# A conversion moves to the second products, and the last expert's splits, transposes and a table load change places, in an attention, MoE and MLP kernel on one core

## The chip, the cores and the metric

The kernel runs on one core of a Trainium2 chip. The metric is the device time of one execution in microseconds. It is taken from runs without a profile; one further execution is profiled, and all rows come from that one.

## What is computed

```python
kv = np.einsum('bhsd,bhse->bhde', k, v); out = np.einsum('bhsd,bhde->bhse', q, kv)
x = out / sqrt(mean(out * out) + 1e-6) * g_norm          # 2304 tokens x 512
noisy = x @ w_gate + log1p(exp(x @ w_noise)) * noise     # 8 experts
top2 = the two largest of each token; weights by softmax over the two
for e in range(8):
    h = np.maximum(x[mask] @ w1[e], 0)                   # 512 -> 1024
    out[mask] += weight * (h @ w2[e])                    # 1024 -> 512
h = out @ w_in; g = h * sigmoid(h); y = g @ w_out        # 512 -> 2048 -> 512
```

q, k, v and the experts' weights are float32. w_in and w_out are float64.

## The kernel before

There are three phases. The attention and the routing end at some 119 us. The experts run from there to 576.6 us, and the MLP from there to the end.

Each product of the experts and of the MLP is made of three passes over split operands. A split takes a float32 tile, rounds it on ScalarE to a high part (h..., such as hw) and subtracts this on VectorE or GpSimd to get the low part (l..., such as lw). Instructions of TensorE, ScalarE and VectorE go through the helper `InOrder` (line 44 of the listing, hence L44 in nearly all rows), which keeps each of the three engines in the order in which the program is written. SyncE (the queue for loads and most stores) and GpSimd are ordered by the compiler's scheduler.

An expert e has 640 places, in five tiles a = 0 to 4 of 128. Its work has two halves.

- First products, `mm1`, for f = 0 to 7: x times a column block of w1, first for places 0 to 255 (part 0, matrices of 256 columns) and then for places 256 to 639 (part 1, 384 columns), 12 matmuls each. ScalarE then writes the high part of h, VectorE the low part (h<-ph in the rows). Beside it, at odd f, w1 of the next expert is split with the subtraction on GpSimd; at even f a conversion runs.
- Second products, `mm2`, for a = 0 to 4: 24 matmuls py, going over f = 0 to 7 with three passes each; the last of the 24 is the one that reads the low part of h of f = 7. After a tile, ScalarE copies py to y and stores it (`store_y`; tiles 0 and 1 go to y_first too). Then follow, by the tables TURN and SPLIT: transposes of gathered rows for the next expert (`Places.turn`: TensorE, then ScalarE for the high part, VectorE for the low part, xT<-xt in the rows), a split of w2 of the next expert (here on VectorE, lw<-rw), and one conversion. Row tile 4 of the next expert is turned inside tile a = 4, before f = 4.

A conversion (`convert`) turns a 128 x 256 block of float64 of w_in or w_out into float32. It has six VectorE instructions in the order bits, bits, unit, w, f, keep, and two on GpSimd: w<-w,bits (L1097), then w<-w,keep (L1098). A store to win_dram or wout_dram and the load of the next float64 block follow on SyncE. There are 64 conversions. Experts 1 to 6 hold five in the first products (f = 0, 2, 4, and two at f = 6) and five in the second, one behind each tile.

The last expert, 7, has no next expert. It splits the first half of w_in (win, four loads of 512 KB from win_dram) in its first products. Then comes `overflow`, a loop with a run-time count for tokens over an expert's room; here the engines go past it. Then the second half of w_in is fetched through the two raw buffers, and split behind tiles 0 (two), 1 and 2. `Block(0)` is the MLP's first block of 256 rows. Its `fetch` gathers two rows per token from y_first into the same raw buffers; `add` weights and adds them on VectorE, `turn` transposes them on TensorE (x2ps) and `split` makes the two parts (x2T). In expert 7, `add(0)`, `turn(0)`, `split(0)` and `add(1)` are written behind tile 3, and row tile 1 is turned inside tile 4 before f = 6. `load_rt(i)` loads the table of places and weights of block i: 16 bytes for each token.

Of the kernel before, what the change touches and what calls it, by code (L numbers as in the profile page):

```python
# [24 lines left out]


TURN = (((), (), (0, 1), (2, 3), ()), ((0, 1), (2,), (3,), (), ()))
SPLIT = ((0, 0, 2, 1, 1), (1, 1, 1, 1, 0), (2, 1, 1, 0, 0))

LOG = (  # L30
    1.7336119413375854, -2.4589619636535645, 1.9598705768585205, -0.5900887250900269, 0.3407464623451233,
# [16 lines left out]
def attention_moe_mlp(  # L48
# [15 lines left out]
    nc = tc.nc  # L64
    pe, act, dve = (InOrder(tc, engine) for engine in (nc.tensor, nc.scalar, nc.vector))
# [13 lines left out]
    NS = CAP // P  # L79
# [112 lines left out]
    def fetch(src, name, shape, raw=None):  # L192
        if raw is None:
            raw = raw_pool[0].tile([P, 1024], F32, tag="raw", name="r" + name, bufs=2)
        nc.sync.dma_start(raw if shape is None else raw.rearrange("p (a b) -> p a b", a=shape), src)
        return raw

    def split(raw, name, high, low):

        hi = wslot("h" + name)  # L200
        lo = wslot("l" + name)
        high.activation(hi, raw, AF.Copy)
        low.tensor_sub(lo, raw, hi.bitcast(F32))  # L203
        return hi, lo
# [13 lines left out]
    def behind(ins):  # L218
        return tc.issue_after(ins.ins) if ins else ExitStack()
# [91 lines left out]

    raw1, raw2, h0 = [], [], []
    listed, marked, stored = {}, {}, []

    def early_y(a, between):

# [10 lines left out]
    with ExitStack() as ph1:  # L327
# [13 lines left out]
        kv, kvT, qT, raw, ss, rinv, logits = {}, {}, {}, {}, {}, {}, {}  # L341
# [632 lines left out]
    def fetch_win(fh):  # L974
        return [
            (fetch(win_dram[c][:, fh * 1024 : (fh + 1) * 1024], f"win{fh}_{c}", None), f"win{fh}_{c}")
            for c in range(KD)
        ]
# [4 lines left out]
    def load_rt(i):  # L983
        s0, s1 = BLOCKS[i]
        rt = mp.tile([P, 4, 4], F32, tag="rt", name=f"rt{i}", bufs=2)[:, : (s1 - s0) // P, :]
        whole = rt_dram[s0:s1, :].rearrange("(t p) c -> p t c", p=P)
        if i:
            nc.sync.dma_start(rt, whole)
        else:
            first = first_dram[s0:s1, :].rearrange("(t p) c -> p t c", p=P)  # L990
            with behind(stored[-1]):
                nc.sync.dma_start(rt[:, :, :TOP], first.bitcast(F32))
                nc.sync.dma_start(rt[:, :, TOP:], whole[:, :, TOP:])
        return rt
# [51 lines left out]
    with ExitStack() as ph2:  # L1046
        tp = ph2.enter_context(tc.tile_pool(name="tp", bufs=2, reuse_waits="tile"))
        tails[0] = tp

        CW = 256  # L1050
        todo = []
        for s0 in range(0, DFF, CW):
            cols = slice(s0, s0 + CW)
            for c in range(KD):
                todo.append((w_in[c * P : (c + 1) * P, cols], win_dram[c][:, cols]))
        for c in range(KFF):
            for s0 in range(0, DM, CW):
                cols = slice(s0, s0 + CW)
                todo.append((
                    w_out[c * P : (c + 1) * P, cols],  # L1060
                    wout_dram[c // 2][(c % 2) * P : (c % 2 + 1) * P, cols],
                ))
        loaded = []

        def load_next():
            if todo:
                src, dst = todo.pop(0)
                raw = tp.tile([P, CW, 2], I32, name="f64", bufs=3)
                nc.sync.dma_start(raw.rearrange("p a b -> p (a b)"), src.bitcast(I32))
                loaded.append((raw, dst))  # L1070


        def convert():
            if not loaded:
                return
            raw, dst = loaded.pop(0)
            top, low = raw[:, :, 1], raw[:, :, 0]
            bits = tp.tile([P, CW], I32, name="bits", bufs=2)
            dve.tensor_scalar(
                bits, top, 3, 0x3FFFFFFF, op0=ALU.logical_shift_left, op1=ALU.bitwise_and  # L1080
            )
            dve.scalar_tensor_tensor(
                bits, top, -0x40000000, bits, op0=ALU.bitwise_and, op1=ALU.bitwise_or
            )
            unit = tp.tile([P, CW], I32, name="unit", bufs=1)
            dve.tensor_scalar(unit, bits, -0x800000, None, op0=ALU.bitwise_and)
            w = tp.tile([P, CW], F32, name="w32", bufs=4)
            dve.scalar_tensor_tensor(
                w, low.bitcast(U32), 2.0**-52, unit.bitcast(F32), op0=ALU.mult, op1=ALU.mult
            )  # L1090
            dve.tensor_scalar(
                top, top, 20, 0x7FF, op0=ALU.logical_shift_right, op1=ALU.bitwise_and
            )

            keep = tp.tile([P, CW], F32, name="keep", bufs=2)
            dve.tensor_scalar(keep, top, 897.0, None, op0=ALU.is_ge)
            nc.gpsimd.tensor_add(w, w, bits.bitcast(F32))  # L1097
            nc.gpsimd.tensor_mul(w, w, keep)  # L1098
            nc.sync.dma_start(dst, w)
            load_next()  # L1100

        def h_tiles(e, f, n):
            return tuple(
                tp.tile([P, CAP], F32R, tag="h", name=f"h{e}_{f}_{l}", bufs=2 * KF)[:, :n] for l in range(2)
            )

        def places(t, s0):
            return lambda a: tuple(x[:, a * P - s0 : (a + 1) * P - s0] for x in t)

        x = Places(0, range(HA // P, NS))  # L1110
        for a in x.tiles:
            x.fetch(a)
        early_y(1, {a + 2: (lambda a=a: x.turn(a)) for a in x.tiles})
        for e in range(E):
            more = e + 1 < E
            now, x = x, Places(e + 1, range(NS))
            if e == 2:
                n_iter = nc.values_load(ntot[0:1, 0:1], min_val=0, max_val=28)
            raw = fetch_w1(e + 1) if more else fetch_win(0)
            got = []  # L1120
            if e == 0:
                w2_sb[0] = []
            parts = (0, 1) if e else (1,)
            s0 = PARTS[parts[0]][0]
            h = []
            for f in range(KF):
                t = h_tiles(e, f, CAP - s0)
                mm1(e, w1_sb[e], now.parts, f, parts, t)
                h.append(places(t, s0))
                if e == 0 and f == 1:  # L1130
                    tiles()
                if f % 2 == more:
                    got.append(split(*raw.pop(0), act, nc.gpsimd if more else dve))
                elif e == 0:
                    w2_sb[0].append(split(raw2[f // 2], f"w2_0_{f // 2}", act, dve))
                elif more:
                    convert()
                    if f == 6:
                        convert()
                if more and f in (2, 4, 6):  # L1140
                    x.fetch(f // 2 - 1)
            if more:
                w1_sb[e + 1] = got
                raw = fetch_w2(e + 1)
                got = w2_sb[e + 1] = []
            else:
                win.update({(0, c): t for c, t in enumerate(got)})
                overflow(n_iter)
                raw = fetch_win(1)
                got = []  # L1150
            if e == 0:
                for _ in range(3):
                    load_next()
            for a in range(s0 // P, NS):
                between = {}
                if a == NS - 1:
                    between = {4: lambda: x.turn(NS - 1)} if more else {6: lambda: (x.turn(1), x.split(1))}
                mm2(e, w2_sb[e], h, a, between)
                if more:
                    for n in TURN[e > 0][a]:  # L1160
                        x.turn(n)
                        if n < 2:
                            x.fetch(n + 3)
                for _ in range(SPLIT[(e > 0) + (not more)][a]):
                    got.append(split(*raw.pop(0), act, dve))
                convert()
                if not more and a == 1:
                    x = Block(0)
                    x.fetch(0)
                    x.fetch(1)  # L1170
                if not more and a == 3:
                    x.add(0)
                    x.turn(0)
                    x.split(0)
                    x.add(1)
            if not more:
                win.update({(1, c): t for c, t in enumerate(got)})
# [5 lines left out]
    with ExitStack() as ph3:  # L1183
# [70 lines left out]
        for i in range(len(BLOCKS)):  # L1254
# [4 lines left out]
            x = Block(i + 1) if i + 1 < len(BLOCKS) else None  # L1259
# [45 lines left out]
```

## Time and profile before

| | |
|---|---|
| median of three runs | 989.76 us (989.26 to 991.65) |
| the profiled execution, its own time | 992.24 us |
| its span, first to last instruction | 990.4 us |
| mean granted clock of TensorE | 0.99 |

In timelines a row has the start from the beginning of the span, the length, the engine, the line and the operation, what it writes and reads with the buffer numbers left out, how many instructions were merged, and in brackets the idle time of the engine before it with what ended it. An engine name with q is its queue: an issue or a wait, no work. PE is TensorE, DVE VectorE, ACT ScalarE, POOL GpSimd, SP SyncE. The name behind an idle time is inferred from semaphores.

### The profile page before, as it was taken

To read this page: it belongs to the slowest core of one execution; us is meant where nothing else is said; L and a number is where in the kernel's file an instruction comes from. 1 tells how busy PE (TensorE), PEld (TensorE's weight loads), DVE (VectorE), ACT (ScalarE), POOL (GpSimd) and SP (SyncE) were. 2 spreads that over 40 slices of the span, in tenths; PEclk is the share of its full clock that TensorE was granted. 3 is DMA by queue.
4 is the path that set the end of the run, shared out by engine and by line. 5 is a ranking of instruction groups with operands and counts; after the bars stand their busy time and mean duration, and the time that the engine had idled before them with its cause. 6 is when DMAs were issued, how large, how long until landed. Compare 5 with 4: busy or idle time off the path is not lost. (4 is left out here: it accounts for less than half of the span.)

```text
span 990.4 us, 14460 instructions
## 1 busy us (share of the span) xinstructions
PE 958.6 (97%) x5586; PEld 819.8 (83%) x5586; DVE 499.0 (50%) x941; ACT 327.5 (33%) x499; POOL 253.1 (26%) x271
## 2 busy tenths in 40 slices
PE   6989999999999999999999999999999999999998
PEld 5877589889798998979888789888888888888886
DVE  2578657676666667576673355232333332232221
ACT  2765254333323323333333243221321231223212
POOL 3000266445455454544520221001100010100000
PEclk9999999999999999999999999999999999999999
DMA  9861737474755638375561472101110020101001
GB/s 325 302 240 45 256 119 237 156 249 128 240 164 187 212 124 282 127 224 186 159 202 51 162 231 86 43 1 43 49 37 21 23 85 1 43 1 43 0 1 44
DMA packets 65096, 127.01 MB, mean 128 GB/s; under 512 B 11264, under 2 KB 19456, under 8 KB 65024
## 3 DMA queue, kind: packets, MB, share of 16 engines
q1 hardware_dynamic: 49392, 91.33, 28.6%
q0 software_dynamic: 6080, 19.93, 6.5%
q10 hardware_dynamic: 9552, 14.79, 4.1%
q8 instruction: 45, 0.74, 0.3%
q14 instruction: 27, 0.22, 0.1%
HBM read 92.94 MB, written 33.08 MB: 127 GB/s over the span
## 5 line engine op out<-in xcount | busy, mean ns | idle before, releaser
L44 PE MATMUL ph<-xT,hw 128*128 128x256 f32 (+1 forms) x960 | 212.5, 312 | 0.1
L44 PE MATMUL py<-hw,h 128*128 128x512 f32 x608 | 200.9, 402 | 7.6 <-DVE h L44 5.5
L44 PE MATMUL pout<-hwout,g 128*128 128x512 f32 x576 | 191.8, 395 | 0.0
L44 PE MATMUL pg<-x2T,hwin 128*128 128x512 f32 (+1 forms) x640 | 184.2, 373 | 0.0
L44 PEld LDWEIGHTS ph<-xT,hw 128*128 128x128 f32 x960 | 162.6, 189 | 1.8 <-DVE xT L44 0.6
L44 DVE TENSOR_TENSOR sg<-pg,sg 128x512 f32<-128x512 f32 x72 | 49.8, 692 | 211.2 <-ACT sg L44 211.2
L44 PE MATMUL ph<-xT,lw 128*128 128x256 f32 (+1 forms) x480 | 149.8, 312 | 0.0
L44 PEld LDWEIGHTS py<-hw,h 128*128 128x128 f32 x608 | 115.2, 189 | 35.8 <-DVE h L44 8.1
L44 PEld LDWEIGHTS pg<-x2T,hwin 128*128 128x128 f32 x640 | 116.6, 189 | 23.4 <-DVE x2T L44 0.2
L44 PEld LDWEIGHTS pout<-hwout,g 128*128 128x128 f32 x576 | 108.2, 188 | 24.3
L44 PE MATMUL py<-lw,h 128*128 128x512 f32 x304 | 120.5, 396 | 0.0
L44 PE MATMUL pg<-x2T,lwin 128*128 128x512 f32 (+1 forms) x320 | 119.0, 372 | 0.0
L44 ACT ACTIVATE sg<-pg 128x512 f32<-128x512 f32 x72 | 43.0, 597 | 217.6 <-PE pg L44 217.6
L44 PE MATMUL pout<-lwout,g 128*128 128x512 f32 x288 | 112.9, 392 | 0.0
L1014 POOL DMA_INDIRECT yg<-y_dram,rt x32 | 31.9, 996 | 260.8 <-PE x2ps L44 219.8
L44 DVE SCALAR_TENSOR_TENSOR h<-ph,h 128x640 fp32r<-128x640 f32 (+1 forms) x64 | 50.5, 789 | 82.6 <-ACT h L44 78.2
L44 ACT ACTIVATE h<-ph 128x640 fp32r<-128x640 f32 (+1 forms) x64 | 43.5, 680 | 144.3 <-PE ph L44 141.4
L44 PEld LDWEIGHTS ph<-xT,lw 128*128 128x128 f32 x480 | 90.6, 189 | 0.0
L1097 POOL TENSOR_TENSOR w<-w,bits 128x256 f32<-128x256 f32 x64 | 47.3, 740 | 145.0 <-DVE w L44 144.7
L44 DVE TENSOR_TENSOR g<-sg,g 128x512 fp32r<-128x512 f32 x72 | 49.8, 692 | 44.7 <-ACT g L44 44.7
L203 POOL TENSOR_TENSOR lw<-rw,hw 128x1024 fp32r<-128x1024 f32 x28 | 67.5, 2410 | 17.0 <-ACT hw L44 17.0
L44 PEld LDWEIGHTS pg<-x2T,lwin 128*128 128x128 f32 x320 | 60.4, 189 | 11.5
(177 smaller groups left out, 1083.6 us busy)
## 6 DMA issues: line engine op xcount, KB each, us to landing
rw<-in_moe_w_dram SPq DMA_DIRECT2D x56, 512.0 KB, 4.1
y_dram<-y ACTq DMA_DIRECT2D x40, 256.0 KB, 4.4
f<-in_moe_w_in_dram SPq DMA_DIRECT2D x32, 256.0 KB, 3.7
f<-in_moe_w_out_dram SPq DMA_DIRECT2D x32, 256.0 KB, 3.3
k<-in_k_dram SPq DMA_DIRECT2D x16, 288.0 KB, 5.9
v<-in_v_dram SPq DMA_DIRECT2D x16, 288.0 KB, 6.0
q<-in_q_dram SPq DMA_DIRECT2D x16, 288.0 KB, 6.3
out_dram<-ob SPq DMA_DIRECT2D x18, 256.0 KB, 3.3
```

Source lines behind the costliest of these rows:

```text
L44: return lambda *args, **kwargs: self.tc.keep_in_program_order(op(*args, **kwargs))
L203: low.tensor_sub(lo, raw, hi.bitcast(F32))
L1014: nc.gpsimd.indirect_dma_start(out=y, out_offset=None, in_=src, in_offset=bass.IndirectOffsetOnAxis(ap=self.rt[:, t, kk : kk + 1].bitcast( ...
L1097: nc.gpsimd.tensor_add(w, w, bits.bitcast(F32))
```

## The change

In experts 1 to 6 the second conversion at f = 6 of the first products goes. In its place there are two conversions behind tile 3 of the second products. Expert 7's two splits behind tile 0 move into tile 0, before f = 3 and before f = 6. Row tile 0 of the MLP is turned and split inside tile 4 before f = 1, no longer behind tile 3, and row tile 1 before f = 5, no longer f = 6. The loads of rt for blocks 1 and up are ordered on SyncE behind the last fetch of w_in.

```diff
-SPLIT = ((0, 0, 2, 1, 1), (1, 1, 1, 1, 0), (2, 1, 1, 0, 0))
+SPLIT = ((0, 0, 2, 1, 1), (1, 1, 1, 1, 0), (0, 1, 1, 0, 0))
@@ fetch
-        nc.sync.dma_start(raw if shape is None else raw.rearrange("p (a b) -> p a b", a=shape), src)
+        fetched.append(
+            nc.sync.dma_start(raw if shape is None else raw.rearrange("p (a b) -> p a b", a=shape), src)
+        )
@@ load_rt
         if i:
-            nc.sync.dma_start(rt, whole)
+            with behind(last_win[0]):
+                nc.sync.dma_start(rt, whole)
@@ first products
                 elif more:
                     convert()
-                    if f == 6:
-                        convert()
@@ expert 7, behind its first products
                 raw = fetch_win(1)
+                last_win.append(fetched[-1])
@@ second products
                 if a == NS - 1:
-                    between = {4: lambda: x.turn(NS - 1)} if more else {6: lambda: (x.turn(1), x.split(1))}
+                    between = {4: lambda: x.turn(NS - 1)} if more else {
+                        1: lambda: (x.turn(0), x.split(0)), 5: lambda: (x.turn(1), x.split(1))
+                    }
+                elif a == 0 and not more:
+                    between = dict.fromkeys((3, 6), lambda: got.append(split(*raw.pop(0), act, dve)))
                 mm2(e, w2_sb[e], h, a, between)
...
                 convert()
+                if e and more and a == 3:
+                    convert()
...
                 if not more and a == 3:
                     x.add(0)
-                    x.turn(0)
-                    x.split(0)
                     x.add(1)
```

## Rows read from the trace of the kernel before

**Rows 1.** The page's busy times: engine, us, share of span, instructions.
```profile
PE 958.6 (97%) x5586; PEld 819.8 (83%) x5586; DVE 499.0 (50%) x941; ACT 327.5 (33%) x499; POOL 253.1 (26%) x271
```
**Rows 2.** TensorE's waits, 130 to 580 us: total us, times, longest us.
```profile
PE py L44 <- DVE h L44: 5.5, 6, 0.9
PE py L44 <- DMA rt<-rt_dram: 2.1, 1, 2.1
```
**Rows 3.** VectorE's timeline, expert 1, end of its first products.
```profile
182.38 0.28 DVE L44 TENSOR_SCALAR bits<-f 128x256 int32<-128x256 int32 x1
182.70 0.43 DVE L44 SCALAR_TENSOR_TENSOR bits<-f,bits 128x256 int32<-128x256 int32 x1
...
184.79 0.28 DVE L44 TENSOR_SCALAR bits<-f 128x256 int32<-128x256 int32 x1
185.11 0.93 DVE L44 SCALAR_TENSOR_TENSOR bits<-f,bits 128x256 int32<-128x256 int32 x1
...
189.79 0.81 DVE L44 SCALAR_TENSOR_TENSOR h<-ph,h 128x640 fp32r<-128x640 f32 x1
```
**Rows 4.** TensorE's timeline, end of expert 1's first tile of second products.
```profile
189.12 0.40 PE L44 MATMUL py<-hw,h 128*128 128x512 f32 x1
189.36 0.39 PE L44 MATMUL py<-lw,h 128*128 128x512 f32 x1
190.66 0.50 PE L44 MATMUL py<-hw,h 128*128 128x512 f32 x1 [0.91 <-DVE h L44]
```
**Rows 5.** VectorE's timeline, from expert 2's last tile into expert 3.
```profile
272.57 0.28 DVE L44 TENSOR_SCALAR bits<-f 128x256 int32<-128x256 int32 x1
...
275.19 0.74 DVE L44 SCALAR_TENSOR_TENSOR xT<-xt,gcol,xT 128x512 fp32r<-128x512 f32 x1
...
277.86 0.66 DVE L44 TENSOR_SCALAR keep<-f 128x256 f32<-128x256 int32 x1
279.59 0.82 DVE L44 SCALAR_TENSOR_TENSOR h<-ph,h 128x640 fp32r<-128x640 f32 x1 [1.07 <-ACT h L44]
```
**Rows 6.** TensorE's timeline there: the first products that read columns 256 to 639.
```profile
276.54 0.51 PE L44 MATMUL ph<-xT,hw 128*128 128x384 f32 x2
```
**Rows 7.** The same place between experts 0 and 1.
```profile
157.03 0.83 PE L44 MATMUL ph<-xT,hw 128*128 128x384 f32 x2
```
**Rows 8.** GpSimd's timeline beside rows 5.
```profile
275.42 0.74 POOL L1098 TENSOR_TENSOR w<-w,keep 128x256 f32<-128x256 f32 x1 [0.29 <-DVE keep L44]
```
**Rows 9.** Stretches: busy us of PE, PEld, DVE, ACT, POOL; granted clock; DMA share; GB/s.
```profile
544.20:547.60 3.40, 3.40 (x8) 2.66 (x9) 0.82 (x1) 0.00 (x0) 0.00 (x0) 0.50 0.88 269
570.00:573.40 3.40, 3.34 (x17) 2.82 (x18) 1.73 (x4) 0.60 (x1) 0.00 (x0) 1.00 0.81 205
```
**Rows 10.** Timelines behind the spare loop: SyncE's first issue, TensorE's first matmul.
```profile
542.29 0.37 SPq L988 DMA_DIRECT2D rt<-rt_dram  x1
...
544.10 0.75 PE L44 MATMUL py<-hw,h 128*128 128x512 f32 x1 [2.14 <-DMA rt<-rt_dram]
```
**Rows 11.** The table rt from 542 to 620 us: issue to landing of its three loads.
```profile
DMA to landing us min/median/max: 3.3/3.7/6.6
```
**Rows 12.** Expert 7's last tiles: timelines of SyncE, GpSimd, VectorE and TensorE.
```profile
555.37 1.46 SPq L195 DMA_DIRECT2D rwin<-win_dram  x2
...
564.15 0.99 POOL L1014 DMA_INDIRECT yg<-y_first,rt  x1 [4.37 <-issue]
...
564.78 1.23 DVE L44 TENSOR_TENSOR lwin<-rwin,hwin 128x1024 fp32r<-128x1024 f32 x1 [3.22 <-ACT hwin L44]
...
569.25 0.75 DVE L44 SCALAR_TENSOR_TENSOR yg<-yg,rt 128x512 f32<-128x512 f32 x1 [0.93 <-DMA yg<-y_first,rt]
...
572.76 0.75 DVE L44 SCALAR_TENSOR_TENSOR yg<-yg,rt 128x512 f32<-128x512 f32 x1 [0.29 <-DMA yg<-y_first,rt]
...
570.06 0.66 PE L44 MATMUL x2ps<-ident,yg 128*128 128x128 f32 x4 [1.83 <-DVE yg L44]
```
**Rows 13.** The two stores to y_first issued at 552.2 and 557.7: issue to landing.
```profile
DMA to landing us min/median/max: 2.1/3.9/5.6
```

More of the change, by code (lines that the diff above doesn't have):

```diff
@@ L313, in attention_moe_mlp @@
     listed, marked, stored = {}, {}, []
+    fetched, last_win = [], []
     def early_y(a, between):
```

## The prediction

> **What bounds the kernel.** I read the busy times first. TensorE is busy for 958.6 us, 97% of the span; VectorE for half of it [rows 1]. So a change counts only where it takes away or makes an idle stretch of TensorE, and the next view is TensorE's waits. In the experts' phase there are eight: six of 0.9 us on the low part of h, which VectorE writes, one of 2.1 put down to the table rt [rows 2], and one of 1.8 on a sum yg of VectorE [rows 12]. The change touches the places of all eight. The third view is VectorE's timeline around them, because VectorE runs in program order: what is written ahead of the awaited instruction delays it.
>
> **The six waits that the change removes.** In expert 1 the first conversion at f = 6 starts at 182.38, the second at 184.79, and the low part of h of f = 7 at 189.79 [rows 3]. The second conversion thus takes 5.00 us against 2.41 for the first. TensorE goes through tile 0 meanwhile. Its last matmul should start 0.23 behind the one at 189.36, the pace of its neighbours, so at 189.59; it starts at 190.66 [rows 4]. The loss is 1.07 us. Without the second conversion the low part could start some 5 us earlier, ahead of its use by far, so the whole loss goes: 6 x 1.07 = 6.4 us.
>
> **What the moved conversion costs where it lands.** It is written behind tile 3, so it stands in VectorE's queue ahead of the low part of row tile 4 of the next expert, which is turned inside tile 4. That is xT, and TensorE waits for it: the second matmul of part 1 in the next expert's first product reads it. How much room is there? From expert 2 into 3, the conversion behind tile 3 starts at 272.57 and xT at 275.19; xT ends at 275.93 [rows 5]. The first two matmuls of part 1 start at 276.54 and 0.18 later [rows 6], so xT is needed at 276.72. The room is 0.79 us. From expert 0 into 1 there is none left already: the same pair spans 0.83 in place of 0.51 us [rows 6, 7].
>
> A conversion is longer than that room. The one alone takes 2.41 us to the start of the next [rows 3]. One right behind another also meets the GpSimd multiplication of that other one. This ran at 275.42 for 0.74 us [rows 8], and the second instruction of the moved conversion would start at about 275.5, inside it. At f = 6 the same meeting made 0.93 us out of 0.43 [rows 3]. So I take 2.41 + 0.50 = 2.91 us. The trace of before shows no second conversion at this very place, so the bounds are: below, 2.41, no meeting; between, 2.59, what the conversion behind xT takes there, from 275.93 to 278.52 [rows 5]; above, the 5.00 of f = 6. The last is far off, since at f = 6 GpSimd also splits w1, and behind tile 3 the split is VectorE's own. 2.91 stands nearest to what I can see of the place.
>
> With 2.91, xT ends at 278.84. TensorE restarts 0.06 later, as it does at 570.06 behind the sum that ends at 570.00 [rows 12], so at 278.90 and not 276.72: 2.18 us at each of six transitions, 13.1 us. With 2.59 it is 11.2, with 2.41 it is 10.1. Nothing is added behind it: VectorE idles 1.07 us ahead of the next low part of h [rows 5], and that one moves back with TensorE.
>
> The Trainium skill (SBUF — State Buffer, section "Who interferes with whom") says that a VectorE instruction with two SBUF inputs contends with a GpSimd one that reads SBUF, and that the second to issue is blocked until the first ends; one with a single input outside the faster modes is not. Of the first two instructions at f = 6 the one with two inputs was stretched, so the trace agrees. By that rule the sum is the one with 2.91; by the undisturbed row it is that with 2.41.
>
> Net of the two parts: 13.1 - 6.4 = +6.7 us. The float64 load and the store that a conversion issues on SyncE move with it. Three blocks are in flight, so the next conversion's block was asked for two conversions earlier, and I cost them at nothing; that distance hides them, and without it each could cost up to a load's few us. On GpSimd the two instructions of the moved conversion pass no gather that TensorE waits for within 2 us.
>
> **Expert 7.** TensorE starts the transposes of row tile 0 at 570.06, after 1.83 us of idle, because the sum of that tile ends at 570.00 [rows 12]. The sum waits for a gather, and the gather for the store of tile 1 to y_first and for a raw buffer. The two stores to y_first landed after 2.1 and 5.6 us [rows 13]. The second, issued at 557.7, runs beside two fetches of w_in issued from 555.37 [rows 12]; it lands at 563.3, and the first gather starts at 564.15 [rows 12]. With the splits inside tile 0, these fetches go out as soon as the earlier halves have landed and are split, some 4 us sooner, and the second store is alone: it lands near 560, and gathers start from 561. The sum then waits on VectorE for the split that ends at 566.01 [rows 12] and is done by 567.5, before the transposes are reached at 568.8. That takes away the wait of some 2.0 us. The sum of row tile 1 now ends at 573.51 [rows 12] and needs a gather that still starts behind 566.01, so I move it up by under a microsecond, to 572.6. TensorE gets there at 571.9, earlier than now, and waits 0.7. Gain 2.0 - 0.7 = 1.3 us. If the store lands no sooner, only the moved places count, 0.6; at most it is 2.0. The two splits now sit ahead of ScalarE's copy of tile 0, some 7 us behind the restart at 544.10 [rows 10]; their loads are issued at once behind the loop, so they should be done by then. If not, the copy and its store are late, which costs at most what is gained here.
>
> **The table load.** The wait of 2.1 us is put down to rt [rows 2], and the stretch behind it runs at a granted clock of 0.50 for 3.40 us [rows 9], which costs 1.7 more. But rt is issued at 542.29 [rows 10] and the quickest of these loads lands after 3.3 us [rows 11], so at 545.6 or later, and TensorE is back at 544.10 [rows 10]. The label is a coincidence; what ends there is the way past the loop. I cost the move of rt at nothing: it is now queued on SyncE behind w_in's fetches, and its first user, block 1, is more than 20 us away.
>
> The Trainium skill (Runtime: NRT & Kernel Launch, section "Instruction fetch mechanics") says that a taken branch to code outside the fetched pages waits for a load of that code. By that rule too the move gains nothing; were the label right, it would gain 3.8.
>
> **The clock.** The idle stretch of 2.14 us was followed by half clock [rows 9, 10], the lower of the two levels, 1.2 in place of 2.4 GHz; that of 1.83 us was not [rows 9, 12]. My new waits would show as about 2.0 us (278.90 less the end of the matmul before, 276.88), between the two. Each that falls on the wrong side costs 3.40 x 0.5 = 1.7 us. The rows don't say where the limit lies, so I count none or one of six in the forecast and leave more to a rival.
>
> **The sum.** +6.7 - 1.3 = +5.4 us, with one stretch at half clock +7.1. The profiled execution has its own time of 992.24, 2.5 above the median of 989.76; the difference goes on the median: 995.2 to 996.9. I predict 996.0 us. Alone, this case reaches from 993 to 999.
>
> **Rivals.** The wait is hidden (faster). VectorE reaches xT before the moved conversion, or makes up for it. For it: VectorE idles half the time [rows 1]. Against it: all rows follow program order, and the room is 0.79 us. That is the point from which it decides: a delay below 0.79 costs nothing. Then -6.4 - 1.3 = -7.7: 982.1 us. Chance 7%.
>
> The conversion meets nothing and costs 2.41: 10.1 - 6.4 - 1.3 = +2.4: 992.2 us. Against it stands the multiplication at 275.42 [rows 8]. 9%.
>
> The label is right, and rt holds up TensorE and the clock: 5.4 - 3.8 = +1.6: 991.4 us. Against it stands the landing. 6%.
>
> The clock falls at most of the transitions, at four: 5.4 + 6.8 = +12.2: 1002.0 us. For it: the new waits are nearer to 2.14 than to 1.83. 14%.
>
> The forecast has 64%.
>
> A measurement of this kernel can tell 0.3%, 3 us. Faster by more: the first rival, 8%. Within: the second, the third and a little of the forecast, 18%. Slower by more: 74%. The range leaves out the first rival and the upper half of the fourth: 990.3 to 1001.0.
>
> **What would show it.** In the profile after, TensorE's waits on the low part of h in tile 0 are gone. In their place stand six of ph on VectorE's xT, of about 2 us, as experts 2 to 7 begin, with two conversions back to back ahead of xT on VectorE. The wait ahead of x2ps in tile 4 falls to under 1 us. The 2.1 us behind the loop stay, perhaps under another name. I am wrong if the six new waits are absent or under 1 us, or if half clock follows each of them.

## The result and the profile after

The changed kernel takes 1003.43 us, the median of five runs (1001.22 to 1005.28). The kernel before, in five runs beside them, takes 991.65 (989.26 to 993.66). The ratio is 1.0111, with an interval of 1.0092 to 1.0130. It is slower, as forecast, but by 11.8 us and not by 5.4 to 7.1; 996.0 was predicted, and the time lies above the range. The profiled execution of after has 1003.43 us as its own time and a span of 1001.6, 11.2 more than before's 990.4.

The busy times of after, which answer to [rows 1]:
```profile
span 1001.6 us, 14459 instructions
PE 962.0 (96%) x5586; PEld 824.5 (82%) x5586; DVE 487.2 (49%) x941; ACT 327.5 (33%) x499; POOL 252.2 (25%) x271
```
TensorE does the same 5586 matmuls and is busy for 3.4 us more. Longer waits don't make an engine busier, so a part of the loss is slower matmuls, a matter of the clock. The rest shows in TensorE's waits from 130 to 590 us (total us, times, longest):
```profile
PE ph L44 <- DVE xT L44: 12.0, 6, 2.1
PE py L44 <- issue: 2.1, 1, 2.1
PE x2ps L44 <- DVE yg L44: 0.3, 1, 0.3
```
The six waits on h of [rows 2] are gone, and six on xT stand in their place. The 2.1 us behind the loop [rows 10] stay, and are no longer put down to rt. The wait of 1.83 ahead of the first x2ps [rows 12] is gone too; the 0.3 is a new one, ahead of the transposes of row tile 1.

VectorE's timeline from expert 2's last tile into expert 3, which answers to [rows 3, 5], with GpSimd's beside it, which answers to [rows 8], and TensorE's, which answers to [rows 6]:
```profile
278.70 0.28 DVE L44 TENSOR_SCALAR bits<-f 128x256 int32<-128x256 int32 x1
279.01 0.93 DVE L44 SCALAR_TENSOR_TENSOR bits<-f,bits 128x256 int32<-128x256 int32 x1
...
281.05 0.64 DVE L44 TENSOR_SCALAR keep<-f 128x256 f32<-128x256 int32 x1
281.61 0.74 DVE L44 SCALAR_TENSOR_TENSOR xT<-xt,gcol,xT 128x512 fp32r<-128x512 f32 x1
...
278.93 0.74 POOL L1102 TENSOR_TENSOR w<-w,keep 128x256 f32<-128x256 f32 x1 [0.29 <-DVE keep L44]
...
280.05 0.34 PE L44 MATMUL ph<-xT,hw 128*128 128x384 f32 x1
282.40 0.44 PE L44 MATMUL ph<-xT,hw 128*128 128x384 f32 x1 [2.01 <-DVE xT L44]
```
The moved conversion runs from 278.70 to xT's start at 281.61, 2.91 us, and its second instruction takes 0.93, while the GpSimd multiplication of the conversion before it runs from 278.93 for 0.74: the numbers of the forecast. (L1102 is the line that was L1098.) TensorE starts a matmul of part 1 at 280.05 and then idles until xT is there.

Stretches of 3.40 us, each right behind one of the six waits, in the columns of [rows 9]:
```profile
220.20:223.60 3.40, 3.39 (x11) 3.39 (x12) 2.31 (x6) 0.00 (x0) 1.62 (x3) 0.51 0.43 130
282.40:285.80 3.40, 3.40 (x23) 3.40 (x24) 2.74 (x7) 0.71 (x1) 1.63 (x3) 1.00 0.39 116
343.10:346.50 3.40, 3.40 (x11) 3.40 (x12) 2.31 (x6) 0.00 (x0) 1.62 (x3) 0.52 0.41 116
405.30:408.70 3.40, 3.40 (x23) 3.40 (x24) 2.74 (x7) 0.70 (x1) 1.62 (x3) 1.00 0.36 125
466.00:469.40 3.40, 3.40 (x11) 3.40 (x12) 2.27 (x6) 0.00 (x0) 1.58 (x3) 0.52 0.39 121
528.00:531.40 3.40, 3.40 (x23) 3.40 (x24) 2.74 (x7) 1.21 (x2) 1.59 (x3) 1.00 0.13 45
```
Behind the first, third and fifth wait the granted clock is 0.51 or 0.52, near the lower level, and TensorE gets through 11 matmuls where it gets through 23 at 1.00. The waits themselves are of much the same length: 2.14, 2.01, 2.02, 2.01, 2.02 and 1.82 us.

The end of expert 7, which answers to [rows 12], in the timelines of GpSimd, VectorE and TensorE:
```profile
575.14 0.99 POOL L1018 DMA_INDIRECT yg<-y_first,rt  x1 [8.52 <-DMA y_first<-y]
...
580.86 0.75 DVE L44 SCALAR_TENSOR_TENSOR yg<-yg,rt 128x512 f32<-128x512 f32 x1 [1.48 <-DMA yg<-y_first,rt]
...
581.75 0.60 PE L44 MATMUL x2ps<-ident,yg 128*128 128x128 f32 x4
585.40 0.66 PE L44 MATMUL x2ps<-ident,yg 128*128 128x128 f32 x4 [0.27 <-DVE yg L44]
```
TensorE is back from the loop at 557.09, so the first gather starts 18.05 us behind that, where it started 20.05 behind 544.10 in before [rows 10, 12]. The transposes of row tile 0 start at 581.75 without a wait; those of row tile 1, at 585.40, wait for 0.27.

Where the 11.2 us are, from TensorE's starts in both traces:

| part | before | after | difference |
|---|---|---|---|
| up to expert 1's first products | 155.60 | 157.54 | +1.9 |
| first second product to the next expert's first product, experts 1 to 6, each (expert 1: 31.40 and 30.23) | 31.28 | 30.10 | 6 x -1.18 = -7.1 |
| first products of expert 2 | 28.19 | 32.10 | +3.9 |
| of 3, 4, 5 and 6 | 28.32 each | 30.60, 32.09, 30.59, 32.09 | +2.3, +3.8, +2.3, +3.8 |
| of expert 7, with its split of w_in | 30.61 | 32.71 | +2.1 |
| expert 7's second products, to the MLP | 32.46 | 30.90 | -1.6 |
| the MLP | 413.84 | 413.58 | -0.3 |

### The profile page after: what moved, and what is told of

It reads as the page before. It is cut to its first block, busy times and chain, and to the rows that moved or that the text cites. A ratio compares the mean times of both kernels' runs of the same rounds, so it can differ in the third digit from the quotient of the medians.

```text
span 1001.6 us, 14459 instructions
## 1 busy us (share of the span) xinstructions
PE 962.0 (96%) x5586; PEld 824.5 (82%) x5586; DVE 487.2 (49%) x941; ACT 327.5 (33%) x499; POOL 252.2 (25%) x271
## 5 line engine op out<-in xcount | busy, mean ns | idle before, releaser
L44 PE MATMUL ph<-xT,hw 128*128 128x256 f32 (+1 forms) x960 | 217.7, 317 | 12.1 <-DVE xT L44 12.0
L44 PEld LDWEIGHTS ph<-xT,hw 128*128 128x128 f32 x960 | 165.9, 192 | 15.4 <-DVE xT L44 14.2
```

Source lines behind the costliest of these rows:

```text
L44: return lambda *args, **kwargs: self.tc.keep_in_program_order(op(*args, **kwargs))
```

## Experiments

In all of them the kernel before ran on the same chip, and the ratio is to its median there: 992.17 us beside the conversion alone, expert 7 alone, the conversion behind tile 1 and after once more; 992.72 beside the first extra VectorE work, the three conversions, the table load alone and the splits alone; 992.94 beside the other four. Each waits row and each stretch is from the one execution of a kernel that is traced.

### Which part loses

The kernel before with the conversion moved and nothing else:
```diff
-                    if f == 6:
-                        convert()
@@ behind a tile of second products
+                if e and more and a == 3:
+                    convert()
```


> Of the change, the moved conversion alone; expert 7 and the table load stay as before. Theory: all of the loss sits here. Six waits of TensorE on xT of 2.0 us (2.2 lost each) take the place of six on h (1.07 lost each), +6.7 us, and some of them are followed by a stretch at half clock of 1.6 us each: three as in the profile after, +11.5 us, with 0 and 6 of them +6.7 and +16. Rival: a good part of the 11 us comes from the table load and expert 7, and this kernel loses less than 5 us.

Measured: 1006.26 us, ratio 1.0145 (1.0105 to 1.0185). Its waits on xT:
```profile
PE ph L44 <- DVE xT L44: 12.0, 6, 2.1
```

And the other way round, after with the conversion back at f = 6:

> Of the change, everything but the moved conversion. Theory: expert 7 gains 1.6 us between its second products and the MLP, as the profile after shows, and the rest of the kernel stays: -1.6 us, same within 0.3%. Rival: the splits ahead of ScalarE's copy, or the table load behind w_in, cost more than they bring: +3 us or more.

Measured: 990.21 us, ratio 0.998 (0.9959 to 1.0001). All of the loss sits in the moved conversion: alone it costs 14 us (10 to 18 by the interval), with the same six waits and the same three stretches at half clock as in after. The edits to expert 7 gain some 2 us, by an interval that just reaches zero. Together that is the 12 of the whole change.

### Is it the conversion or its place

After with the second conversion behind tile 1, not tile 3:
```diff
-                if e and more and a == 3:
+                if e and more and a == 1:
```


> As the changed kernel, but the second conversion stands behind tile 1 of the second products and not behind tile 3. Theory: only the place behind tile 3 lies ahead of an xT that is needed soon; behind tile 1 the xT that it delays is needed two tiles later. Both kinds of waits go: -6.4 - 1.6 = -8 us against before, no half clock at a transition. Rival: VectorE has no room for the sixth conversion anywhere in the second products, and the waits on xT stay, at 1 us or more: 0 us or slower.

Measured: 984.44 us, ratio 0.9918 (0.9890 to 0.9946). TensorE's waits:
```profile
PE py L44 <- issue: 2.1, 1, 2.1
PE x2ps L44 <- DVE yg L44: 0.7, 1, 0.7
PE ph L44 <- DVE xT L44: 0.3, 1, 0.3
```
The work is the same and the waits on h and on xT are gone but for 0.3 us. So the place decides, as the argument from VectorE's program order has it. But the room of 0.79 us is used up here: from expert 2 into 3, xT ends at 279.09 and the matmul that reads it starts at 279.15. So, one tile earlier:
```diff
-                if e and more and a == 3:
+                if e and more and a == 0:
```


> As the kernel with the conversion behind tile 1, but behind tile 0. Behind tile 1 it pushed the chain of VectorE on until the xT of the next expert was just in time (220.56 for a use at about 220.5, one wait of 0.28 us showed). Theory: one tile earlier the room of 0.79 us ahead of xT is back, no wait on xT at any of the six transitions: 0.3 to 1 us faster than behind tile 1, -8 to -9 us against before. Rival: the six instructions stand in the way of something else there (the row tiles 0 and 1 of the next expert) and it is slower than behind tile 1.

Measured: 981.98 us (979.54 to 987.82), ratio 0.9897 (0.9869 to 0.9925), 11.0 below before and some 21 below after. Its waits:
```profile
PE py L44 <- issue: 2.1, 1, 2.1
PE ph L44 <- DVE xT L44: 0.4, 1, 0.4
```
The timelines of VectorE and TensorE from expert 2 into 3:
```profile
271.41 0.74 DVE L44 SCALAR_TENSOR_TENSOR xT<-xt,gcol,xT 128x512 fp32r<-128x512 f32 x1
...
272.76 0.51 PE L44 MATMUL ph<-xT,hw 128*128 128x384 f32 x2
```
xT ends at 272.15, and the second of the two matmuls needs it 0.18 behind 272.76, at 272.94: the 0.79 of [rows 5, 6] is back, and the pair again takes 0.51. None of the six transitions has a wait; the 0.4 stands between experts 0 and 1, where the change has no edit. Against before the span is 11.3 us shorter: 7.1 are the waits on h, 3.1 lie in expert 7's second products (29.33 in place of 32.46), and 1.7 lie ahead of expert 1; some 0.6 are lost elsewhere. Of the 3.1 some 1.5 are the stretch at half clock behind the loop, which before's profile has [rows 9] and this one hasn't.

### Does the clock's pattern hold

After once more, unchanged:

> The changed kernel once more. Theory: the six waits come back to within 0.15 us, since VectorE's order sets them, but how many of them are followed by half clock, and which, differs from the profile after (second, fourth and sixth wait not, first, third and fifth yes): something beside the length of the wait decides. Rival: the length decides alone, and the same three transitions are slow again.

Measured: 1002.55 us, ratio 1.0110 (1.0071 to 1.0149). The waits are 2.14, 2.01, 2.02, 2.01, 2.02 and 1.82 us again, and half clock follows the first, third and fifth again. That the pattern would differ was wrong: it comes again with the same kernel.

### How long a wait is followed by half clock

The conversion behind tile 1, and extra VectorE work that nobody reads ahead of xT:
```diff
-                if e and more and a == 3:
+                if e and more and a == 1:
                     convert()
+                if e and more and a == 3:
+                    junk = tp.tile([P, CW], I32, name="unit", bufs=1)
+                    for half in range(2):
+                        dve.tensor_scalar(
+                            junk[:, half * P : (half + 1) * P].bitcast(F32), iota_f, 1.0, None, op0=ALU.mult
+                        )
+                    for _ in range(5):
+                        dve.tensor_scalar(junk, junk, -0x800000, None, op0=ALU.bitwise_and)
```


> The conversion behind tile 1 as in the run before, and behind tile 3 of experts 1 to 6 some 2 us of idle work for VectorE ahead of xT (two small products and five of 256 columns, nobody reads them). Theory: xT is late by 2.0 - 0.79 us, so six waits that show as about 1.1 us (1.3 lost): +7.8 us against the kernel with the conversion behind tile 1, so about 0 against before, and none is followed by half clock, since 0.9 and 1.8 us were not in the profile of before. Rival: what makes the clock fall is the place, not the length, and some of the six are followed by half clock here too, 1.6 us each.

Measured: 1003.65 us, ratio 1.0110 (1.0083 to 1.0137). The size was missed: the extra work took 2.34 us and not 2.0, and the room was spent, so the waits became 2.28, 2.20, 2.63, 2.25, 2.22 and 1.91, longer than after's. They still tell something. Half clock follows the first, the second and the fifth. The stretches behind the second, of 2.20, and behind the third, the longest:
```profile
281.20:284.60 3.40, 3.40 (x11) 3.40 (x12) 2.13 (x6) 0.00 (x0) 1.46 (x2) 0.55 0.28 90
344.10:347.50 3.40, 3.40 (x24) 3.40 (x25) 2.57 (x7) 0.70 (x1) 1.48 (x2) 1.00 0.27 91
```
So in this range the longer wait is not the one that the clock falls behind. The next kernel has the conversion behind tile 0, where the room is, and four of the last instruction:
```diff
+                if e and more and a == 0:
...
+                    for _ in range(4):
```


> The conversion behind tile 0, and behind tile 3 of experts 1 to 6 idle work for VectorE of 0.39 + 4 x 0.40 = 2.0 us ahead of xT, as measured in the first try, which had 2.3 us and met no room of 0.79. Theory: the six waits show as about 1.1 us (1.25 lost): +7.5 us against the kernel with the conversion behind tile 0, about -1 against before, and none is followed by half clock. Rival: the place decides and not the length, and two or three of the six are followed by half clock, 1.6 us each.

Measured: 992.71 us, ratio 0.9999 (0.9976 to 1.0021). Against the kernel with the conversion behind tile 0 that is +10.7 and not +7.5: the six waits lost 1.4 us each and not 1.25, and half clock follows the loop in this profile and not in that one. The waits are 1.26, 1.15, 1.14, 1.13, 1.15 and 0.96. Their row among the waits:
```profile
PE ph L44 <- DVE xT L44: 6.8, 6, 1.3
```
The first two of the six stretches behind them; the other four also have 1.00:
```profile
217.80:221.20 3.40, 3.40 (x23) 3.40 (x24) 2.59 (x7) 0.71 (x1) 1.49 (x2) 1.00 0.33 111
277.60:281.00 3.40, 3.40 (x23) 3.40 (x24) 2.57 (x7) 0.70 (x1) 1.48 (x2) 1.00 0.25 83
```
None of these six waits is followed by half clock. To the other side, with tile 2's conversion behind tile 3 as well, so that three stand there:
```diff
-                convert()
+                if not (e and more and a == 2):
+                    convert()
                 if e and more and a == 3:
                     convert()
+                    convert()
```


> As the changed kernel, but the conversion behind tile 2 of experts 1 to 6 also moves behind tile 3, so that three stand there. Theory: xT is late by another 2.9 us, six waits that show as 4.9 us (5.1 lost), 30.6 - 6.4 - 1.6 = +22.6 us, and now each of the six is followed by half clock, since no place of so long a wait avoids it: another 6 x 1.6, +32 us. Rival: half clock follows three of the six again, +27 us.

Measured: 1026.61 us, ratio 1.0335 (1.0308 to 1.0361). The waits' row, in which a seventh, short one is counted:
```profile
PE ph L44 <- DVE xT L44: 29.6, 7, 5.0
```
The stretches behind the second, fourth and sixth transition, the three that kept their clock in after:
```profile
292.20:295.60 3.40, 3.40 (x12) 3.40 (x13) 2.22 (x6) 0.00 (x0) 1.53 (x3) 0.54 0.39 116
422.40:425.80 3.40, 3.40 (x11) 3.40 (x12) 2.26 (x6) 0.00 (x0) 1.57 (x3) 0.53 0.38 118
552.20:555.60 3.40, 3.40 (x11) 3.40 (x12) 2.27 (x6) 0.00 (x0) 1.58 (x3) 0.54 0.12 39
```
A third conversion adds 2.9 us to each wait, and waits of 4.7 to 5.0 us are followed by half clock six times in six.

Last, the conversion moved in experts 4 to 6 alone:
```diff
-                if e and more and a == 3:
+                if e > 3 and more and a == 3:
@@ first products
+                    if f == 6 and e < 4:
+                        convert()
```


> The changed kernel, but the conversion moves only in experts 4 to 6; experts 1 to 3 keep two at f = 6. Three waits of 2.2 us lost stand for three of 1.07: +3.3 - 1.6 = +1.7 us, and half clock on top. In the changed kernel the first, third and fifth of six transitions were followed by half clock in each of three profiles. Theory: it is not the transition but where its wait falls in time, so with all three transitions some 8 us earlier the pattern of the last three (no, yes, no) changes. Rival: it belongs to the transition itself (the work beside it), and only the one from 5 into 6 is followed by half clock, +3.3 us.

Measured: 997.87 us, ratio 1.0042 (1.0020 to 1.0064). Three waits on xT are left, 2.01, 2.02 and 1.83 us, with these stretches behind them:
```profile
398.30:401.70 3.40, 3.40 (x14) 3.40 (x15) 2.25 (x6) 0.32 (x1) 1.57 (x3) 0.64 0.39 124
460.50:463.90 3.40, 3.40 (x11) 3.40 (x12) 2.30 (x6) 0.00 (x0) 1.61 (x3) 0.53 0.44 136
522.60:526.00 3.40, 3.40 (x23) 3.40 (x24) 2.74 (x7) 1.21 (x2) 1.60 (x3) 1.00 0.14 44
```
Yes, yes, no, where after has no, yes, no at the same places. So the clock's answer isn't tied to the place either: the transition from expert 4 into 5 has the same wait, 2.01 us, and another answer once the transitions ahead of it have no such wait. It also comes 7 us earlier in the execution, as the theory wanted; the run doesn't tell the two apart.

### The parts of expert 7

The table load alone moved behind w_in's last fetch (the edits at `fetch`, `load_rt` and `last_win`):

> Of the change, only the order of the table load behind w_in. Theory: nothing; TensorE's idle stretch of 2.1 us behind the loop stays to within 0.1 us under another name. Rival: the table load held TensorE up, the stretch falls under 1 us and the stretch at half clock behind it goes, -3.8 us.

Measured: 993.92 us, one run. The wait behind the loop:
```profile
PE py L44 <- issue: 2.1, 1, 2.1
```
The stretch of 3.40 us behind that wait:
```profile
546.95:550.35 3.40, 3.40 (x15) 2.79 (x16) 0.82 (x1) 0.00 (x0) 0.00 (x0) 1.00 0.69 249
```
The stretch lost is 2.14 us with the load as without it; only its label changes. The label was a coincidence, and the move is worth nothing here. What does hold TensorE for the 2.14 us no run varied.

The splits alone (the new row of SPLIT, and `between` for tile 0):

> Of the change, only the two splits inside expert 7's first tile. Theory: the fetches of w_in go out earlier, the store of tile 1 to y_first lands within 4 us in place of 5.6, and the idle stretch ahead of the transposes of row tile 0 falls from 1.83 us to under 0.3: -1.5 us from the second products' start to the MLP. Rival: the gather is held by something else, and the stretch stays over 1.5 us.

Measured: 989.42 us, one run. The landing of the two stores to y_first, from issue on:
```profile
DMA to landing us min/median/max: 3.3/3.4/3.5
```
The wait ahead of the first x2ps:
```profile
PE x2ps L44 <- DVE yg L44: 0.3, 1, 0.3
```
The transposes and splits of the MLP's rows alone (the new `between` of tile 4, and the two calls behind tile 3 gone):

> Of the change, only the places of the two row tiles' transposes in expert 7's last tile. Theory: the sum of row tile 0 ends where it did, TensorE does 0.7 us of products first, so the stretch of 1.83 us ahead of the transposes falls to about 1.1, and from the second products' start to the MLP 0.6 us are gained. Rival: the gain of 1.6 us is due to these places, and the splits did nothing more.

Measured: 993.3 us, one run, with this wait ahead of the first x2ps:
```profile
PE x2ps L44 <- DVE yg L44: 1.1, 1, 1.1
```
The two single times tell little, so I read the stretch from TensorE's return to the MLP's first product. It is 32.46 us in before with half clock at its start, and 31.0 with the table alone, where the clock stays up. The splits alone make it 29.34, the turns alone 30.47. So the splits gain 1.7 us and the turns 0.5. They don't add up: with both, and the table load, the stretch is 29.54 in the profile of expert 7 alone, no shorter than with the splits.

## Why the prediction was wrong

| term | predicted | in the traces |
|---|---|---|
| six waits on the low part of h | -6.4 | -7.1 |
| six waits on xT | +13.1 | +13.6 |
| half clock behind them | 0 to +1.7 | +4.5 |
| expert 7 | -1.3 | -1.6 |
| the table load | 0 | 0 |
| ahead of expert 1 | not in the sum | +1.9 |
| MLP | not in the sum | -0.3 |
| sum | +5.4 to +7.1 | +11.0 (the spans: +11.2) |

The 13.6 is the six differences of first products, 18.1, less three times 1.5, by which the slow ones (32.10, 32.09, 32.09) stand above the plain ones (30.60, 30.59).

**The step that failed** is the one on the clock: "The rows don't say where the limit lies, so I count none or one of six". Three of six came, in the profiles of after and of its repeat, at 1.5 us each and not 1.7. The mechanism was seen and its price was nearly right; the count was wrong. I read 1.83 (not followed) and 2.14 (followed) as two sides of one limit, and then counted waits of 2.0 as if they were mostly on the safe side. The runs show no such limit between them: 2.01 is followed in the last-three kernel and not in after, 2.20 is and 2.63 is not in one and the same kernel, and the 2.14 behind the loop is followed in before and not with the table load moved. Two rows that disagree gave no reason for one rather than three; three at the prediction's own price would have made +5.4 + 5.1 = +10.5 on the median, 1000.3 us. The rival with four has the nearest time, 1002.0, but by luck: it has one stretch too many, each 0.2 too dear, and that 2.3 us happens to fill in for what the next paragraph names.

**The rest of the miss** is not a step of the argument. In the two profiles 1.9 us went ahead of expert 1, where the change has no edit. Expert 0's first products start between 117.2 and 124.2 us over the profiles of this case, so a pair of executions can differ by that. And the median of before was 989.76 in three runs and is 991.65 in five; the prediction was counted on the former. How many stretches at half clock the other executions of after had is not known: one is traced, and the mean granted clock of the five runs goes from 0.983 to 0.986.

**What was right.** The conversion behind tile 3 stands ahead of xT in VectorE's queue; it takes 2.91 us, not 2.41; the room of 0.79 us is all that hides. That room was read at one transition; over the six of before it goes from 0.66 to 0.97, and so the first wait is 2.14 and the last 1.82. The rivals "hidden" and "meets nothing" fall with the six waits of 2.0 us and the 0.93 of the second instruction. The rule of the Trainium skill (SBUF — State Buffer, section "Who interferes with whom"), by which the instruction with two SBUF inputs is the one that contends, held at the new place: 0.93 us, where the same instruction meets nothing it takes 0.42 or 0.43.

The waits on h cost 1.18 us each and not 1.07. Expert 7 came out nearly by the steps given: with the splits alone in tile 0 the second store lands in 3.5 us and not 5.6 [rows 13], the wait of 1.83 is gone in after, and the new one on row tile 1 is 0.27 where 0.7 was forecast. The rival "label right" falls with the table-load kernel.

**What stays open.** Beside a wait's length something decides whether half clock follows a wait of about two us. It repeats in a kernel, and it changed when the transitions before were changed. The theory of the last-three kernel, that the time at which a wait falls decides, is a rival that no run refutes and none isolates. One sign speaks for it. In the kernel with waits of 1.1 us TensorE is back from the loop at 545.81, works at the full clock, and the clock falls only some 1.5 us later:
```profile
545.81:547.27 1.46, 1.46 (x6) 1.24 (x7) 0.15 (x1) 0.00 (x0) 0.00 (x0) 1.00 0.86 269
547.30:550.70 3.40, 3.40 (x9) 2.67 (x8) 0.92 (x1) 1.82 (x2) 0.00 (x0) 0.50 0.33 136
```
Behind the first wait of after the clock is down as soon as TensorE works again (0.51 from 220.20 on). So the fall isn't bound to the wait's end. Nor was it tried to keep the moved conversion where it is and to let xT go ahead of it.

## What to carry to other kernels

Before background work is moved on an in-order engine, look up the next instruction behind its new place that the bottleneck waits for, and the room that this one has: here 0.79 us of room against 2.91 us of work made a gain of 7 us into a loss of 12, and three tiles earlier the same work cost nothing. Price a wait of the bottleneck with the clock in it; by the counts of this case, near 1 us the wait alone, near 2 us the wait and half of what a half-clock stretch costs, near 5 us both in full. A releaser's name on a wait is a guess that one run can refute; here the landing time of the transfer spoke against it before any run.

## What the runs showed of the hardware

I had expected a limit in the length of the wait, above which the clock falls. Over these kernels half clock followed none of six waits on xT of 0.96 to 1.26 us, 14 of 27 of 1.8 to 2.7 us (after, its repeat and the conversion alone with the same three of six, so these are not separate draws; three of six with the waits of 1.9 to 2.6; two of three), and all six of 4.7 to 5.0 us. In the middle group the length doesn't order the cases. A stretch at half clock cost some 1.5 us where it can be set beside one at full clock, at the transitions of after (32.09 against 30.60) and behind the loop (32.46 against 31.0). The loop's wait, 2.10 to 2.14 us in every profile, was followed by it in 8 of 14.
